# The last K-transposed-V slice padded from 64 to 128 rows, its four pairs in one place, and routing one step later

## Chip, cores and metric

The kernel runs on one core of one Trainium2 chip. The metric is the device time of one execution in microseconds (us); lower is better.

## What is computed

Three layers follow one another on 4608 tokens (8 batches of 576) of width 512. In the reference, cut to what matters:

```python
kv = np.einsum('bhsd,bhse->bhde', k, v)          # linear attention, 8 heads of 64
out = np.einsum('bhsd,bhde->bhse', q, kv)
x = out / sqrt(mean(out * out, -1) + 1e-06) * g_norm
h = np.maximum(np.maximum(x @ w1, x @ w2), x @ w3)   # first MoE: 512 -> 768 -> 512
x = h @ w_out
noisy_logits = x @ w_gate + log1p(exp(x @ w_noise)) * noise   # second MoE: 8 experts
# the two best experts of each token, with weights from their logits
h = np.maximum(x[mask] @ w1[e], 0.0)
out[mask] += top2_w[mask, k, None] * (h @ w2[e])
```

## The kernel before

The tokens go through the first two layers in nine chunks of 512 (`c` = 0 to 8). Each engine runs its instructions in the order in which the program text issues them; tiles and semaphores decide only how long one waits.

A chunk has 18 steps (`g` = 0 to 17), and then a window. In step `g` the function `g1` makes one product for the first MoE: 12 matmuls of 128 rows and 512 columns into one of four PSUM banks (`hbank`, used in turn). ScalarE (ACT) or VectorE (DVE) then empties the bank into `hm`: line 307 for the first of three products, line 309 for the other two, and lines 312 and 313 split the result into a high and a low part. So a bank that a product took is wanted again four bank requests later. The window holds the second product of the first MoE (`g2`, line 327), and the attention output of the next chunk (`ao`, `norm`, `xtrans`).

`misc1(c, g)` is called ahead of each `g1(c, g)` and puts the other work of a chunk between the steps:

- Step 0: the loads of `q` of the next chunk and of K and V of batch `c + 1`. A batch has 576 rows, which are four slices of 128 and a last one of 64 rows. Two slices go to the tile `KV0`, two to one of the three tiles `STG` (named `G` in the profile), and the 64 rows to another. `stage` hands out the three in turn.
- Step 1: `route_a` of the chunk before: DVE finds the two best experts of each token, and their one-hot sums `Mb` and `Cb` (lines 365 to 368).
- Step 3: `route_b`: two small bf16 matmuls on PE (lines 379 and 380) count the tokens, and DVE makes row numbers from them (lines 382 to 386). `scatter(c - 1, 0)` behind it has GpSimd (POOL) issue four indirect DMAs (line 393) that write the rows of the first choice to `Xg`.
- Step 7: `scatter(c - 1, 1)` for the second choice. It begins with a DVE copy into `rows` (line 401), the tile that the first four DMAs read.
- Steps 8, 9, 11 and 12: `kv_pair(c + 1, p, ...)`, five fp32 matmuls for each of four pairs of heads (line 180), which are ten instructions on PE. The fifth is the 64-row slice. `kv_out` after step 12's pair copies the result to `KB`.
- Steps 14 and 16: `ao` and `norm` for half of the next chunk.

Chunk 0 also converts the first MoE's weights from float64 (`conv_a`, `conv_b`: lines 417 to 435, on DVE, ACT and POOL), and holds batch 1's matmuls: slices 0 to 3 ahead of steps 3 to 6, the 64-row slice ahead of step 9, with all four pairs side by side. Batch 0 stands in the prologue, slice by slice. The three tiles `STG` are also used by `gate_a` and `gate_b` in chunk 0's window (lines 445 to 458). `fills` issues POOL's instructions that set `tri` and `base`, and then the DMA that fills `out` with zeros (line 496) and a part of `Xg` (line 498); it stands at chunk 1, step 0, but POOL has little else to do then and runs ahead.

The second MoE (phase 2) follows with a table of work units that is built at run time, and the experts' products on PE (lines 900, 914 and 947).

Of the kernel before, what the change touches and what calls it, by code (L numbers as in the profile page):

```python
# [17 lines left out]
NB, NH, S, D = 8, 8, 576, 64  # L18
# [57 lines left out]
def unit_order():  # L76
    seq = [("S", 0), ("S", 1), ("4", 0)]
    small = [("1", i) for i in range(N1_MAIN)] + [("2", i) for i in range(N2)]
    for i in range(1, N4):
        seq.append(("4", i))  # L80
        seq.append(small.pop(0))
    return seq + small, [("1", i) for i in range(N1_MAIN, N1)]


def body(tc, A, dbg=None):
    nc = tc.nc
    PE, ACT, DVE, POOL, SP = nc.tensor, nc.scalar, nc.vector, nc.gpsimd, nc.sync
# [8 lines left out]
    def st(name, shape, dt=F):  # L96
        return sb.tile(shape, dt, name=name)
# [4 lines left out]
    STG = [st(f"G{i}", [128, 2048]) for i in range(3)]  # L102
# [5 lines left out]
    XN = [st(f"xn{i}", [128, 512]) for i in range(3)]  # L108
# [17 lines left out]
    def abank():  # L126
        cnt["a"] += 1
        return AC[(cnt["a"] - 1) % 4]

    def C(name, a=0, b=None):  # L130
        lo, hi = CST[name]
        return cst[:, lo + a:hi if b is None else lo + b]

    ident = C("ident")

# [1 line left out]
    stg_n = [0]  # L137

    def stage(src, width=2048, parts=128):
        t = STG[stg_n[0] % 3]  # L140
        stg_n[0] += 1
        SP.dma_start(t[0:parts, 0:width], src)
        return t

    ACT.preload_act_table_set(LNEXP)
    kvraw = {}

    def quarters(t):
        return [t[:, i * 512:(i + 1) * 512] for i in range(4)]

    def load_kv(b, part):
        if part == 0:
            SP.dma_start(KV0, A["kv4"][b, 0])
            kvraw[b] = [quarters(KV0)]
        elif part == 1:
            kvraw[b].append(quarters(stage(A["kv4"][b, 1])))
        else:
            t = stage(A["kvr"][b], 1024, 64)
            kvraw[b].append((t[0:64, 0:512], t[0:64, 512:1024]))

    qbuf = [RB, KV0] + [RB] * 7

# [3 lines left out]
    def load_q(c):  # L166
        SP.dma_start(qbuf[c][:, 0:2048], A["qT"][c])

    DVE.memset(KB[0], 0.0)
    POOL.memset(KB[1], 0.0)  # L170
    POOL.memset(ones, 1.0)

# [1 line left out]
    def kv_mm(b, p, s, out):  # L174
        r = kvraw[b]
        if s < 4:
            k, v = r[s // 2][2 * (s % 2):2 * (s % 2) + 2]
        else:
            k, v = r[2]
        PE.matmul(out, k[:, p * 128:(p + 1) * 128], v[:, p * 128:(p + 1) * 128], start=s == 0, stop=s == 4)  # L180

    def kv_pair(b, p, bank):
        for s in range(5):
            kv_mm(b, p, s, bank[:, p * 128:(p + 1) * 128])

    def kv_out(b, bank):
        v = bank.rearrange("p (a e) -> p a e", a=4)
        for h in range(2):
            s = slice(h * 64, h * 64 + 64)
            (ACT.copy if h else DVE.tensor_copy)(KB[b % 2][s, :, s], v[s, :, s])  # L190
# [75 lines left out]
        xtrans_hi(i, t)  # L266
        xtrans_lo(i, t)

# [1 line left out]
    def split(src, w):  # L270
        ACT.activation(w[:, 0:1024], src, AF.Copy)  # L271
        DVE.tensor_tensor(w[:, 1024:2048], src, w[:, 0:1024].bitcast(F), op=OP.subtract)  # L272
# [16 lines left out]
    first = []  # L289
# [41 lines left out]
            for z in range(2):  # L331
                ACT.activation(rows[:, i, z * 256:z * 256 + 256], x2b[i][z][:, 0:256], AF.Copy)

# [1 line left out]
    lgs = st("lgs", [128, 4, 16])  # L335
    nl = st("nl", [128, 4, 8])
    m8 = st("m8", [128, 4, 8])
# [64 lines left out]
        for i in range(4):  # L402
            scatter_to(si[c % 2][:, 4 * k + i:4 * k + i + 1], rows[:, i, :])

# [1 line left out]
    w_raw = {}  # L406

    def load_w1(s):
        t = STG[stg_n[0] % 3]
        stg_n[0] += 1  # L410
        SP.dma_start(t.bitcast(U64), A["w1s"][s])
        w_raw[s] = t.rearrange("p (n t) -> p n t", t=2)
# [27 lines left out]
    def gate_a(j, ring):  # L440
        t, d = wsrc(9 + j), STG[j]
        for ff in range(2):
            TR = ring()
            for k in range(4):
                PE.transpose(TR[:, k * 128:(k + 1) * 128], t[:, ff * 512 + k * 128:ff * 512 + (k + 1) * 128], ident)
            ACT.activation(d[:, ff * 512:ff * 512 + 512], TR, AF.Copy)
# [10 lines left out]
        ACT.activation(hi, t, AF.Copy)  # L457
        DVE.tensor_tensor(lo, t, hi.bitcast(F), op=OP.subtract)

# [1 line left out]
    pad = st("pad", [128, XW])  # L461
    load_kv(0, 0)
    stg_n[0] = 2
    load_kv(0, 1)
    stg_n[0] = 1
    load_kv(0, 2)
    load_q(0)
    stg_n[0] = 0
    load_w1(0)
    SP.dma_start(cst, A["cst"][:, 0:CST["tri"][0]])  # L470
    SP.dma_start(gn, A["gn"])
# [11 lines left out]
    def kv_diag(b):  # L483
        for p in range(4):
            for h in range(2):
                s = slice(h * 64, h * 64 + 64)
                (ACT.copy if h else DVE.tensor_copy)(KB[b][s, p, s], AC[p][s, s])
# [3 lines left out]
    def fills():  # L491
        POOL.tensor_copy(tri, pad[:, 0:128])
        POOL.tensor_copy(base, C("eR"))
        POOL.memset(pad[:, 0:513], 0.0)
        DVE.tensor_copy(pad[:, 513:514], C("trash"))
        POOL.dma_start(A["out"].rearrange("(a p) f -> p a f", p=128),
                       pad[:, 0:512].unsqueeze(1).to_broadcast([128, OUT_ROWS // 128, 512]))
        POOL.dma_start(Xg[DUMMY:DUMMY + 512, :].rearrange("(a p) w -> p a w", p=128),
                       pad.unsqueeze(1).to_broadcast([128, 4, XW]))
# [29 lines left out]
    def conv_some(b, upto=0):  # L529
        budget[0] += b  # L530
        while conv and (budget[0] >= conv[0][0] or (conv_b, upto) in [x[1:] for x in conv]):
            t, f, k = conv.pop(0)
            budget[0] -= t
            f(k)
            if f is conv_b and k + 3 < 12:
                load_w1(k + 3)

# [1 line left out]
    P2 = {}  # L539
    order, rest = unit_order()  # L540
    NUN = len(order)
    state = {"split": 0, "load": 3, "g2done": -1, "NP": 4 * NUN}
# [86 lines left out]
            load_pair(state["load"])  # L629
            state["load"] += 1  # L630

# [1 line left out]
    def misc1(c, g):  # L633
        if c == 1 and g == 0:
            fills()
        if c == 0:
            if g == 16:
                assert 9 not in [x[2] for x in conv] and conv
                gate_a(0, abank)
            conv_some(CB if g < 17 else 99.0, g // 2)  # L640
            if 3 <= g < 7:
                for p in range(4):
                    if g == 3:
                        abank()
                    kv_mm(1, p, g - 3, AC[p][:, 0:128])
            if g == 5:
                kvraw[1].append([XN[z][0:64, :] for z in range(2)])
                for z in range(2):
                    SP.dma_start(XN[z][0:64, :], A["kvr"][1][:, z * 512:z * 512 + 512])
            if g == 6:  # L650
                load_q(1)
            if g == 9:
                for p in range(4):
                    kv_mm(1, p, 4, AC[p][:, 0:128])
                kv_diag(1)
        if g == 0:
            SP.dma_start(noise[c % 2], A["noise"][c])
        if g == 0 and 0 < c < NCH - 1:
            load_q(c + 1)
            if c + 1 < NB:  # L660
                for i in range(3):
                    load_kv(c + 1, i)
        if c > 0:
            if g == 1:
                route_a(c - 1)
            if g == 3:
                route_b(c - 1)
                scatter(c - 1, 0)
            if g == 7:
                scatter(c - 1, 1)  # L670
        if 0 < c < NB - 1:
            for p, gg in enumerate((8, 9, 11, 12)):
                if g == gg:
                    if p == 0:
                        P2["kvb"] = abank()
                    kv_pair(c + 1, p, P2["kvb"])
                    if p == 3:
                        kv_out(c + 1, P2["kvb"])
        if 0 < c < NCH - 1 and g in (14, 16):
            ao(c + 1, (g - 14) // 2, abank())  # L680
            norm(c + 1, (g - 14) // 2)
        if c == NCH - 1:
            if g == 5:
                spec_pick()
                load_regs(0, spi[0:1, 0:1], spi[0:1, 1:2])
                regE[1] = regE[0]
                regS[1] = SP.value_load(spi[0:1, 2:3], min_val=0, max_val=DUMMY)
                for p in range(3):
                    load_pair(p)
            if g == 9:  # L690
                load_rows(0)
            if g in (12, 13, 14, 15, 16, 17):
                splits(1)
# [56 lines left out]
            g1(c, g)  # L750
        window(c)

# [1 line left out]
    c = NCH - 1  # L754
    TS = STG[(stg_n[0] + 2) % 3]

# [107 lines left out]
        x = ui[u]  # L864
        load_regs(u, tabi[0:1, 0, x:x + 1], tabi[0:1, 1, x:x + 1])

# [1 line left out]
    hring = B1.rearrange("p (f a t) -> p f a t", f=4, a=2)  # L868
    hn = [0]
    h1 = [sb2.tile([128, 2, 256], FR, name=f"h1_{i}") for i in range(2)]  # L870
# [205 lines left out]
```

## Time and profile before

| | |
|---|---|
| device time, median of 3 runs | 1648.06 us (1647.77 to 1648.1) |
| span of the profiled execution, first to last instruction | 1651.1 us |
| mean granted TensorE clock | 0.982 |
| PE busy | 1593.1 us (96%) |
| PE weight loads | 1363.3 us (83%) |
| DVE, ACT, POOL busy | 749.0, 608.3, 278.3 us |
| DMA | 219.38 MB, mean 133 GB/s |

The profiled execution is one of its own: its span is 3.0 us longer than the median of the runs, and no device time of its own is listed. Times in rows are counted from the start of that span. PE counts as busy from a matmul's start to its modelled end, and matmuls overlap, so what one of them takes on PE is read from the distance to the next one's start. Chunk 1 starts at about 154 us, chunk 8 ends at about 775 us.

### The profile page before, as it was taken

The page shows a single profiled execution, that of the slowest core. Times are in us where ns is not written, and L with a number is a line of the kernel's source. Part 1 is how long each engine was busy: PE and PEld are TensorE (multiplying, and loading weights), DVE is VectorE, ACT ScalarE, POOL GpSimd, SP SyncE. Part 2 cuts the span into 40 slices and gives each one's busy share as a digit, 9 for nine tenths or more (in the row PEclk, how much of TensorE's full clock was granted, in tenths as well). Part 3 has the DMA queues.
Part 4 walks back from the last instruction along what each step waited for, and adds up shares of the span by engine and source line. Part 5 has one row for each costly group of instructions (what it writes and reads, how often), then busy time and mean ns, then how long its engine had stood idle before and what let it go on. Part 6 is the DMA issues. An engine that isn't in the chain of part 4 may idle for free. (4 is left out here: it accounts for less than half of the span.)

```text
span 1651.1 us, 21416 instructions
## 1 busy us (share of the span) xinstructions
PE 1593.1 (96%) x8500; PEld 1363.3 (83%) x8500; DVE 749.0 (45%) x1369; ACT 608.3 (37%) x968; POOL 278.3 (17%) x271
## 2 busy tenths in 40 slices
PE   6779999999999999999999999999999999999996
PEld 5659898988888888989788888888888888888885
DVE  6973243434333333444644355364354444544442
ACT  4443131313222222333233355454354443544433
POOL 3770201111020202020311121111020110201102
PEclk8978999999999999999999999999999999999998
DMA  7428121202030301051464575675574654746543
GB/s 269 155 87 313 52 84 51 103 33 110 26 129 7 135 8 71 1 179 37 188 191 115 141 217 164 196 208 166 154 212 132 179 166 145 219 130 183 165 122 71
DMA packets 53000, 219.38 MB, mean 133 GB/s; under 512 B 6944, under 2 KB 7200, under 8 KB 35488
## 3 DMA queue, kind: packets, MB, share of 16 engines
q1 hardware_dynamic: 33040, 166.50, 28.7%
q0 software_dynamic: 19856, 51.48, 13.3%
q8 instruction: 68, 1.11, 0.3%
q14 instruction: 36, 0.29, 0.1%
HBM read 166.49 MB, written 51.47 MB: 132 GB/s over the span
## 5 line engine op out<-in xcount | busy, mean ns | idle before, releaser
L287 PE MATMUL bank<-B,W 128*128 128x512 f32 x1944 | 466.2, 397 | 12.4 <-ACT W L434 6.8
L287 PEld LDWEIGHTS bank<-B,W 128*128 128x128 f32 x1944 | 364.2, 190 | 93.8 <-ACT W L434 10.6
L947 PE MATMUL bank<-W,B 128*128 128x512 f32 x1728 | 422.4, 391 | 2.0 <-issue 1.5
L947 PEld LDWEIGHTS bank<-W,B 128*128 128x128 f32 x1728 | 320.0, 188 | 67.8 <-issue 2.4
L900 PE MATMUL bank<-B,W 128*128 128x512 f32 (+1 forms) x1728 | 361.0, 346 | 0.0
L900 PEld LDWEIGHTS bank<-B,W 128*128 128x128 f32 x1728 | 275.7, 189 | 40.2
L272 DVE TENSOR_TENSOR W<-G,W 128x1024 fp32r<-128x1024 f32 x200 | 242.5, 1224 | 132.1 <-ACT W L271 132.1
L905 DVE SCALAR_TENSOR_TENSOR B<-bank,B 128x512 fp32r<-128x512 f32 (+1 forms) x176 | 104.3, 593 | 266.3 <-ACT B L904 265.8
L271 ACT ACTIVATE W<-G 128x1024 fp32r<-128x1024 f32 x200 | 207.6, 1054 | 47.1 <-PE bank L947 39.5
L904 ACT ACTIVATE B<-bank 128x512 fp32r<-128x512 f32 (+1 forms) x176 | 91.6, 521 | 351.2 <-PE bank L900 344.1
L327 PE MATMUL bank<-W,B 128*128 128x256 f32 (+1 forms) x1296 | 172.9, 291 | 4.0 <-ACT W L457 2.8
L327 PEld LDWEIGHTS bank<-W,B 128*128 128x128 f32 x1296 | 164.6, 192 | 5.5 <-ACT W L457 3.0
L393 POOL DMA_INDIRECT Xg<-RA,si x72 | 70.1, 973 | 566.2 <-ACT hm L307 458.7
L309 DVE TENSOR_TENSOR hm<-hm,bank 128x512 f32<-128x512 f32 x108 | 73.9, 684 | 162.1 <-PE bank L287 150.1
L953 POOL DMA_INDIRECT out<-xn,idt x37 | 59.6, 1612 | 318.6 <-ACT xn L952 178.9
L312 ACT ACTIVATE B<-hm 128x512 fp32r<-128x512 f32 x54 | 34.0, 630 | 214.1 <-DVE hm L309 195.2
L900 PE MATMUL bank<-xlo,W 128*128 128x512 f32 x384 | 105.0, 394 | 0.0
L900 PEld LDWEIGHTS bank<-xlo,W 128*128 128x128 f32 x384 | 72.0, 187 | 16.6
L602 ACT ACTIVATE B<-bank 128x512 fp32r<-128x512 f32 x76 | 45.3, 596 | 68.5 <-PE bank L598 61.7
L953 POOL DMA_INDIRECT out<-x2T,idt x19 | 30.6, 1611 | 233.4 <-ACT x2T L952 175.8
L313 DVE TENSOR_TENSOR B<-hm,B 128x512 fp32r<-128x512 f32 x54 | 43.0, 796 | 39.8 <-ACT B L312 39.1
L307 ACT ACTIVATE hm<-bank 128x512 f32<-128x512 f32 x54 | 32.2, 597 | 71.9 <-PE bank L287 62.6
(175 smaller groups left out, 1055.2 us busy)
## 6 DMA issues: line engine op xcount, KB each, us to landing
G<-mw SPq DMA_DIRECT2D x100, 1024.0 KB
RB<-Xg SPq DMA_DIRECT2D x13, 1028.0 KB
G<-w1s SPq DMA_DIRECT2D x12, 1024.0 KB
out<-pad POOLq DMA_DIRECT2D x1, 9472.0 KB
kv<-kv SPq DMA_DIRECT2D x8, 1024.0 KB
RB<-qT SPq DMA_DIRECT2D x8, 1024.0 KB
G<-kv SPq DMA_DIRECT2D x7, 1024.0 KB
RA<-Xg SPq DMA_DIRECT2D x8, 514.0 KB
```

What stands on the lines that cost most here:

```text
L271: ACT.activation(w[:, 0:1024], src, AF.Copy)
L272: DVE.tensor_tensor(w[:, 1024:2048], src, w[:, 0:1024].bitcast(F), op=OP.subtract)
L287: PE.matmul(bank, w[:, a, k, s], xT[b][:, k, :], start=n == 0 and k == 0, stop=n == 2 and k == 3)
L309: DVE.tensor_tensor(hm, hm, bank, op=OP.max)
L327: PE.matmul(x2b[i][z][:, 0:hi - lo], h[:, a, s], w[:, b, lo:hi], start=f == 0 and n == 0, stop=f == 5 and n == 2)
L393: i = POOL.indirect_dma_start(out=Xg, out_offset=bass.IndirectOffsetOnAxis(ap=idx, axis=0), in_=src, in_offset=None)
L602: ACT.activation(x[0][:, :, s], t, AF.Copy)
L900: PE.matmul(bank[:, 0:n], w[:, a, k, s], x[b][:, k, 0:n], start=z == 0, stop=z == 11)
L904: ACT.activation(h[:, 0, 0:n], bank[:, 0:n], AF.Relu)
L905: DVE.scalar_tensor_tensor(h[:, 1, 0:n], bank[:, 0:n], 0.0, h[:, 0, 0:n].bitcast(F), op0=OP.max, op1=OP.subtract)
L947: PE.matmul(obank[i], h[:, a, s], w[:, b, ff % 2, :], start=ff == 0 and n == 0, stop=ff == 7 and n == 2)
L953: POOL.indirect_dma_start(out=A["out"], out_offset=bass.IndirectOffsetOnAxis(ap=idt[u % 3][:, i:i + 1], axis=0), in_=y, in_offset=None, co ...
```

## The change

The 64-row slice becomes a slice of 128 rows. The upper 64 rows of the tiles that hold it are set to zero: by POOL for `STG[1]` at the program's start (batch 0), by DVE for the two `XN` tiles in chunk 0's step 5 (batch 1), and by POOL for `STG[2]` at chunk 1's step 0, ahead of `fills` (batches 2 to 7). So that the zeros stay, the loads of batches 2 to 7 no longer take the next tile in turn: the slices 2 and 3 go to `STG[0]` or `STG[1]`, the last one to `STG[2]`. The four pairs of batches 2 to 7 stand together ahead of step 10. `route_b` and the scatters move from steps 3 and 7 to 4 and 8.

```diff
--- before.py
+++ after.py
...
@@ -153,10 +153,13 @@
             SP.dma_start(KV0, A["kv4"][b, 0])
             kvraw[b] = [quarters(KV0)]
         elif part == 1:
-            kvraw[b].append(quarters(stage(A["kv4"][b, 1])))
+            t = STG[2 if b == 0 else b % 2]
+            SP.dma_start(t, A["kv4"][b, 1])
+            kvraw[b].append(quarters(t))
         else:
-            t = stage(A["kvr"][b], 1024, 64)
-            kvraw[b].append((t[0:64, 0:512], t[0:64, 512:1024]))
+            t = STG[1 if b == 0 else 2]
+            SP.dma_start(t[0:64, 0:1024], A["kvr"][b])
+            kvraw[b].append((t[:, 0:512], t[:, 512:1024]))
 
     qbuf = [RB, KV0] + [RB] * 7
 
@@ -166,11 +169,12 @@
     def load_q(c):
         SP.dma_start(qbuf[c][:, 0:2048], A["qT"][c])
 
+    POOL.memset(STG[1][64:128, 0:1024], 0.0)
     DVE.memset(KB[0], 0.0)
     POOL.memset(KB[1], 0.0)
     POOL.memset(ones, 1.0)
 
     def kv_mm(b, p, s, out):
         r = kvraw[b]
         if s < 4:
...
@@ -457,15 +461,12 @@
         ACT.activation(hi, t, AF.Copy)
         DVE.tensor_tensor(lo, t, hi.bitcast(F), op=OP.subtract)
 
     pad = st("pad", [128, XW])
     load_kv(0, 0)
-    stg_n[0] = 2
     load_kv(0, 1)
-    stg_n[0] = 1
     load_kv(0, 2)
     load_q(0)
-    stg_n[0] = 0
     load_w1(0)
     SP.dma_start(cst, A["cst"][:, 0:CST["tri"][0]])
     SP.dma_start(gn, A["gn"])
@@ -535,8 +536,7 @@
             if f is conv_b and k + 3 < 12:
                 load_w1(k + 3)
 
-    P2 = {}
     order, rest = unit_order()
     NUN = len(order)
     state = {"split": 0, "load": 3, "g2done": -1, "NP": 4 * NUN}
@@ -629,9 +629,10 @@
             load_pair(state["load"])
             state["load"] += 1
 
     def misc1(c, g):
         if c == 1 and g == 0:
+            POOL.memset(STG[2][64:128, 0:1024], 0.0)
             fills()
         if c == 0:
             if g == 16:
@@ -644,8 +645,9 @@
                         abank()
                     kv_mm(1, p, g - 3, AC[p][:, 0:128])
             if g == 5:
-                kvraw[1].append([XN[z][0:64, :] for z in range(2)])
+                kvraw[1].append([XN[z][:, :] for z in range(2)])
                 for z in range(2):
+                    DVE.memset(XN[z][64:128, :], 0.0)
                     SP.dma_start(XN[z][0:64, :], A["kvr"][1][:, z * 512:z * 512 + 512])
             if g == 6:
                 load_q(1)
@@ -663,19 +665,16 @@
         if c > 0:
             if g == 1:
                 route_a(c - 1)
-            if g == 3:
+            if g == 4:
                 route_b(c - 1)
                 scatter(c - 1, 0)
-            if g == 7:
+            if g == 8:
                 scatter(c - 1, 1)
-        if 0 < c < NB - 1:
-            for p, gg in enumerate((8, 9, 11, 12)):
-                if g == gg:
-                    if p == 0:
-                        P2["kvb"] = abank()
-                    kv_pair(c + 1, p, P2["kvb"])
-                    if p == 3:
-                        kv_out(c + 1, P2["kvb"])
+        if 0 < c < NB - 1 and g == 10:
+            bank = abank()
+            for p in range(4):
+                kv_pair(c + 1, p, bank)
+            kv_out(c + 1, bank)
         if 0 < c < NCH - 1 and g in (14, 16):
             ao(c + 1, (g - 14) // 2, abank())
             norm(c + 1, (g - 14) // 2)
...
@@ -864,7 +863,7 @@
         x = ui[u]
         load_regs(u, tabi[0:1, 0, x:x + 1], tabi[0:1, 1, x:x + 1])
 
     hring = B1.rearrange("p (f a t) -> p f a t", f=4, a=2)
     hn = [0]
     h1 = [sb2.tile([128, 2, 256], FR, name=f"h1_{i}") for i in range(2)]
```

PE's order in chunk 1, the stretch with the pairs. `G` are the `STG` tiles, `kv` is `KV0`; a row here is one fp32 matmul (two instructions in the profile), and `waits` names the engine or DMA queue whose semaphore it waits for. Before:

```order
L287 MATMUL bank_105<-B_84,W_73 128x512 [waits DVE_49]
L287 MATMUL bank_105<-B_84,W_73 128x512 x11
L180 MATMUL bank_111<-kv_91 128x128 x2
L180 MATMUL bank_111<-G_81 128x128 x2
L180 MATMUL bank_111<-G_82 128x128
L287 MATMUL bank_106<-B_84,W_73 128x512 [waits DVE_49]
L287 MATMUL bank_106<-B_84,W_73 128x512 x11
L287 MATMUL bank_107<-B_84,W_74 128x512 [waits Activation_49]
L287 MATMUL bank_107<-B_84,W_74 128x512 x11
L180 MATMUL bank_111<-kv_91 128x128 x2
L180 MATMUL bank_111<-G_81 128x128 x2
L180 MATMUL bank_111<-G_82 128x128
```

Of the change:

```order
L184 MATMUL bank_111<-kv_91 128x128 x2
L184 MATMUL bank_111<-G_81 128x128 x2
L184 MATMUL bank_111<-G_83 128x128
L184 MATMUL bank_111<-kv_91 128x128 x2
L184 MATMUL bank_111<-G_81 128x128 x2
L184 MATMUL bank_111<-G_83 128x128
L291 MATMUL bank_107<-B_84,W_74 128x512 [waits Activation_49]
L291 MATMUL bank_107<-B_84,W_74 128x512 x11
```

The last slice is the `G_82` row of a pair before and the `G_83` row now. Before, one product of 12 matmuls or two stand between two pairs (here the second and the third); now the four pairs follow one another (here the third and the fourth), and step 10's product comes behind them. Only the first pair waits for its loads, before and now.

PE's order in chunk 1 around the routing. Before:

```order
L287 MATMUL bank_105<-B_84,W_69 128x512 x12
L287 MATMUL bank_106<-B_84,W_70 128x512 x12
L379 LDWEIGHTS onesb
L379 MATMUL bank_107<-Cb,onesb 128x40 [waits DVE_49]
L380 LDWEIGHTS trib [waits Pool_49]
L380 MATMUL bank_107<-Mb,trib 128x32
L287 MATMUL bank_104<-B_84,W_70 128x512 [waits Activation_49]
L287 MATMUL bank_104<-B_84,W_70 128x512 x11
L287 MATMUL bank_105<-B_84,W_71 128x512 [waits DVE_49]
L287 MATMUL bank_105<-B_84,W_71 128x512 x11
```

Of the change:

```order
L291 MATMUL bank_106<-B_84,W_70 128x512 x12
L291 MATMUL bank_107<-B_84,W_70 128x512 x12
L383 LDWEIGHTS onesb [waits DVE_49]
L383 MATMUL bank_104<-Cb,onesb 128x40 [waits Activation_49]
L384 LDWEIGHTS trib [waits Pool_49]
L384 MATMUL bank_104<-Mb,trib 128x32
L291 MATMUL bank_105<-B_84,W_71 128x512 [waits DVE_49]
L291 MATMUL bank_105<-B_84,W_71 128x512 x11
L291 MATMUL bank_106<-B_84,W_71 128x512 [waits DVE_49]
L291 MATMUL bank_106<-B_84,W_71 128x512 x11
```

One more product stands ahead of the routing's matmul, the wait for DVE has moved to the weight load ahead of it, and the routing takes the bank of the chunk's first product (emptied by ACT). Step 4's product now takes the bank of the second one, which DVE empties.

POOL's order at the end of chunk 0's conversions and at `fills`. Before:

```order
L435 TENSOR_TENSOR W_79<-RA,W_79 128x2x512 [waits Activation_49]
L435 TENSOR_TENSOR W_80<-RA,W_80 128x2x512 [waits Activation_49]
L492 CAST trib<-pad 128x128 [waits DMAHW0_49]
L493 COPY base<-cst 128x8 [waits DMAHW5_49]
L494 MEMSET pad 128x513 [waits Pool_49]
L496 DMA out<-pad 128x37x512 [waits Pool_49]
L498 DMA Xg<-pad 128x4x514 [waits DVE_49]
```

Of the change:

```order
L439 TENSOR_TENSOR W_79<-RA,W_79 128x2x512 [waits Activation_49]
L439 TENSOR_TENSOR W_80<-RA,W_80 128x2x512 [waits Activation_49]
L635 MEMSET G_83 64x1024 [waits PE_49,Activation_49,Pool_49]
L493 CAST trib<-pad 128x128 [waits DMAHW0_49,Pool_49]
L494 COPY base<-cst 128x8 [waits DMAHW5_49]
L495 MEMSET pad 128x513 [waits Pool_49]
L497 DMA out<-pad 128x37x512 [waits Pool_49]
L499 DMA Xg<-pad 128x4x514 [waits DVE_49]
```

POOL's memset of `STG[2]` (`G_83`), which waits for PE, stands ahead of the instructions of `fills`.

## Rows read from the trace of the kernel before

**Rows 1.** The page: PE's busy time; PE's clock in 40 slices, in tenths.

```profile
PE 1593.1 (96%) x8500; PEld 1363.3 (83%) x8500; DVE 749.0 (45%) x1369; ACT 608.3 (37%) x968; POOL 278.3 (17%) x271
...
PEclk8978999999999999999999999999999999999998
```

**Rows 2.** Windows, one chunk: stretch, length, PE, PEld, DVE, ACT, POOL busy; clock; DMA.

```profile
155.90:234.80 78.90, 78.49 (x453) 68.58 (x452) 29.06 (x85) 20.29 (x43) 8.51 (x16) 1.00 0.22 82
```

**Rows 3.** Waits of PE: us in total, times, the longest.

```profile
PE bank L379 <- DVE Cb L368: 3.3, 8, 0.4
```

**Rows 4.** Timeline of PE, first and last 64-row place (start, us); group of those rows.

```profile
175.55 0.61 PE L180 MATMUL bank<-kv 128*128 128x128 f32 x4
176.32 0.28 PE L180 MATMUL bank<-G 128*128 128x128 f32 x1
176.53 0.37 PE L180 MATMUL bank<-G 64*128 64x128 f32 x1
176.74 0.27 PE L180 MATMUL bank<-G 64*128 64x128 f32 x1
176.94 0.50 PE L287 MATMUL bank<-B,W 128*128 128x512 f32 x1
177.28 0.39 PE L287 MATMUL bank<-B,W 128*128 128x512 f32 x1
...
586.73 0.27 PE L180 MATMUL bank<-G 64*128 64x128 f32 x1
587.26 0.39 PE L287 MATMUL bank<-B,W 128*128 128x512 f32 x1
...
L180 PE MATMUL bank<-G 64*128 64x128 f32 x56 | 12.8, 317 | 0.0
```

**Rows 5.** Timeline of PE, 64-row passes of batch 0.

```profile
11.43 0.94 PE L180 MATMUL bank<-G 64*128 64x128 f32 x7
```

**Rows 6.** Timeline of PE, routing of chunk 0 and the ninth routing.

```profile
160.77 0.61 PE L287 MATMUL bank<-B,W 128*128 128x512 f32 x2
161.79 0.18 PE L379 MATMUL bank<-Cb,onesb 128*128 128x40 bf16 x1 [0.41 <-DVE Cb L368]
161.84 0.48 PE L287 MATMUL bank<-B,W 128*128 128x512 f32 x1
...
778.77 0.39 PE L947 MATMUL bank<-W,B 128*128 128x512 f32 x1
779.07 0.48 PE L900 MATMUL bank<-B,W 128*128 128x512 f32 x1
```

**Rows 7.** Timeline of DVE, step 1 of chunk 1.

```profile
162.72 0.68 DVE L309 TENSOR_TENSOR hm<-hm,bank 128x512 f32<-128x512 f32 x1
```

**Rows 8.** Timeline of DVE and POOL: start, chunk 0, and line 313 in chunk 1.

```profile
0.94 0.48 DVE L169 MEMSET kvbd<- 128x512 f32 x1 [0.94 <-PEq L1068]
...
58.82 0.67 DVE L309 TENSOR_TENSOR hm<-hm,bank 128x512 f32<-128x512 f32 x1
59.03 2.45 POOL L421 TENSOR_TENSOR G<-RB,G 128x1024 int32<-128x1024 int32 x1 [1.21 <-issue]
60.64 1.38 DVE L313 TENSOR_TENSOR B<-hm,B 128x512 fp32r<-128x512 f32 x1 [1.14 <-ACT B L312]
...
164.89 0.69 DVE L313 TENSOR_TENSOR B<-hm,B 128x512 fp32r<-128x512 f32 x1 [0.70 <-ACT B L312]
```

**Rows 9.** Timeline of POOL, PE, DVE around the fill; windows: last three clock, DMA, GB/s.

```profile
120.31 2.19 POOL L496 DMA_DIRECT2D out<-pad  x1 [0.33 <-POOL pad L494]
133.48 1.85 PE L453 MATMUL bank<-wgn,G 128*128 128x16 f32 x16
174.29 0.17 DVE L401 COPY RA<-wt 128x4 f32<-128x4 f32 x1 [1.91 <-DMA Xg<-RA,si]
...
125.00:130.00 5.00, 5.00 (x25) 5.00 (x25) 0.19 (x1) 1.37 (x3) 0.00 (x0) 0.50 1.01 374
145.00:150.00 5.00, 5.00 (x45) 5.00 (x43) 2.99 (x6) 2.09 (x5) 0.00 (x0) 1.00 1.01 419
```

## The prediction

> **What bounds the kernel now.** I read the page first, then PE's waits, the stages by windows, and only then single instructions. PE is busy for 1593.1 us of the span, and its clock is below full speed only in the first four slices (digits 8, 9, 7, 8) and the last one [rows 1]. The windows show a middle chunk: PE busy in 78.49 of 78.90 us at clock 1.00, DMA at 0.22 [rows 2]. So in chunks 1 to 8 a microsecond taken from PE's instructions or waits comes off the end, as long as no other wait appears. In the list of waits only one belongs to these chunks: line 379, 3.3 us in 8 times, released by DVE's `Cb` [rows 3]. Chunk 0 is another stage: there DVE and POOL convert weights, and PE's own time is worth little.
>
> The 0.41 us before `Cb` was known. What the list of waits does not show is the price of the 64-row slice: PE counts as busy there, and one must read start times.
>
> **The 64-row slice.** Batches 2 to 7 have four pairs each, so 24 places where two 64-row passes (an fp32 matmul is two instructions) stand between 128-row work. In the first one the 128-row passes start 0.11 us apart (seven steps from 175.55 to 176.32). Then: 0.21 to the first 64-row pass, 0.21 to the second, 0.20 to the next product's matmul, and 0.34 to the one after that [rows 4]. Together 176.32 to 177.28, 0.96 us. With 128 rows I expect three steps of 0.11 and one of a 512-column matmul, 0.22 to 0.23 (two of them take 0.61, one 0.39 [rows 6]): 0.56 us. The excess is 0.40 us. The last place shows the same: 586.73 to 587.26 is 0.53, and in the first place 176.74 to 177.28 is 0.54. The group of 56 rows is 28 matmuls, 4 of them of batch 0, which leaves the 24 [rows 4]. 24 x 0.40 = 9.6, with rounding 9.4 to 9.6; I take **9.5 us**.
>
> Do 128 rows cost more per pass than 64? In batch 0 the 64-row passes stand together: seven starts within 0.94 us, of which the last one's 0.27 goes off, so 0.11 us a step [rows 5], as with 128 rows. The padded passes cost nothing by this row.
>
> The Trainium skill, TensorEngine Tiling (Array Packing), section Theoretical Speedup, speaks against the change: a dimension of at most 64 can bring up to a factor of two by tiling, which padding would give up. By that rule the 64 passes would be dearer by half a step each, 3.5 us in all. Rows 5 do not bear it out, since these 64-row passes all sit on the same rows of the array and none overlaps another.
>
> **The four pairs together.** They move from before steps 8, 9, 11 and 12 to before step 10. Forty passes at 0.11 us are 4.4 us in one piece, no more than in four. The loads they need are issued at the chunk's start, so the first pair gets two steps more (5.5 us) of time. The copy to `KB` comes two steps earlier, and its readers stay at step 14. Alone, this part is worth nothing.
>
> **Routing one step later.** Before: the last matmul ahead of it starts at 160.99 (160.77 plus 0.22), the next product's at 161.84: 0.85 us, with 0.41 of idle put down to `Cb` [rows 6]. The ninth routing, in the second MoE, has no wait: 778.77 to 779.07, 0.30 us [rows 6]. So one costs 0.55 us more than it must. One more product (12 x 0.23 = 2.7 us) ahead of it covers that five times. 8 x 0.55 = **4.4 us**. The DVE instructions behind the routing stood behind line 313 of step 2 anyway (164.89 to 165.58 [rows 8]), 3 us after PE's routing, so tables and scatters keep their times.
>
> **Chunk 0.** The prologue's four last matmuls lose about 0.2 us on the chain to the first copies of `KB` (two steps of 0.21 that become 0.11): **-0.2**. Batch 1's group at step 9 saves PE as much, which waits for the conversions there: nothing. POOL's memset of `G` at the start is hidden, since PE reads it only after 11 us [rows 5]. DVE gets two memsets of 64x512 ahead of line 309 of step 5. The nearest row is 0.48 us for 128x512 [rows 8]; two are 0.97. Line 309 starts at 58.82, line 313 at 60.64 and ends at 62.02, because POOL's addition holds until 61.48; undisturbed, line 313 takes 0.69 [rows 8]. Shifted by 0.97 it starts at 61.61, after POOL's end, and ends at 62.30: **+0.3**. That is one end. The other: the second memset, too, waits for POOL's end; then line 309 starts at about 61.95, line 313 at 63.77, ending at 64.46: +2.4. I take the first, because line 309 itself runs beside the same POOL instruction in 0.67 us [rows 8], and a memset reads less than it.
>
> The Trainium skill, SBUF — State Buffer, section Who interferes with whom, has the rule for it: a DVE instruction with at most one SBUF input, outside the two-port modes, does not contend with GpSimd. By it the term is 0.3; if memset were in such a mode it would be 2.4. No row shows a DVE memset beside a POOL instruction that reads.
>
> **The fill of `out`.** POOL's memset of `STG[2]` must wait for `gate_b(2)`, which reads that tile until 133.48 + 1.85 = 135.33 [rows 9]. Behind it in POOL's queue stand `tri`, `base`, `pad` and the fill, now issued at 120.31 [rows 9]. With about 1 us for the memset (twice the columns of the 0.48) and about 1.7 for the small ones (an estimate: 0.5 for a memset of 513 columns, the rest alike) it goes out at 138, 18 us later, and its data, after an issue of 2.19, from about 141. 9.7 MB of `out`, 1.05 of `Xg` and 2.4 MB of loads of batch 2 run at 374 GB/s or a little more [rows 9]: 35 us, to about 176. The scatters of chunk 0 stand behind it in the same queue and land by about 179. Who waits for them: DVE's copy of `rows` (1.91 us already now, at 174.29 [rows 9]), at step 8 instead of 7. PE's step 8 ends near 177.7 (step 4 begins at 164.0, see the rivals, and five steps take 13.7); its bank is wanted again at step 12, at about 190 (step 9, 4.4 us of pairs, steps 10 and 11). Ten microseconds of cover: nothing. `tri` is ready at 138, and is wanted at 164.
>
> **Sum.** -9.5 -4.4 -0.2 +0.3 = -13.8 us. The profiled span of 1651.1 would be 1637.3. The runs have a median of 1648.06, 3.0 us under that span; the terms are PE time at full clock and carry over, so 1648.06 - 13.8 = **1634.3 us**.
>
> **Rivals.**
> *The excess is not of the 64 rows* but of the change of tile or the semaphores there. Against: 128-row passes step from `kv` to `G` without a break [rows 4]. Then only routing gains: 1643.8.
> *Routing's wait comes back a step later*, on the bank: step 4's product now takes the bank that line 309 of step 1 empties at 162.72 + 0.68 = 163.40 [rows 7]. PE gets there at 161.84 - 0.55 + 2.7 = 164.0. Half a microsecond of room; if it is used up in all chunks, 4.4 come back: 1638.7.
> *Chunk 0 is dearer*: the memset takes its upper end (+2.1), and a stretch of chunk 0 at 1.2 instead of 2.4 GHz grows with it. The three microseconds between the profiled execution and the runs suggest some 2 us for that: 1638.4.
> *The padding costs* the 3.5 us of the tiling rule as a mechanism of the array: 1637.8.
> *Slower, by one mechanism*: the late fill. If fill and loads move at half the rate, the scatters land at about 141 + 70 = 211, DVE stands at the copy until then, and PE waits for step 8's bank from 190 on: 21 us, so 1655. From 204 on this decides the sign. The trace has 1.01 of DMA share and 419 GB/s with both kinds of transfer in flight [rows 9], which speaks against it.
>
> **How the numbers follow.** The forecast gets 0.78, chunk 0 dearer 0.12, the wait on the bank 0.04, the excess elsewhere 0.03, the padding 0.01, the late fill 0.02. The range: the forecast less up to 3 us, because chunk 0's half-speed stretches may also shrink (estimate from the same 3.0 us), and up to chunk 0's dear case: 1631.3 to 1638.6. A measurement here tells 0.2%, 3.3 us, from nothing. All cases but the last stay below 1644.8, only the excess elsewhere comes near: faster 0.95, same 0.03, slower 0.02.
>
> **What would show it.** After: no step over 0.13 us within the forty passes, the first product's matmul behind them 0.11 later and then 0.23 apart; chunks 1 to 6 shorter by 4 x 0.40 + 0.55 = 2.1 us (78.9 to 76.8), chunks 7 and 8 by 0.55; no wait at the routing in PE's list, and none at step 4; line 313 after the memsets ending 0.3 later; the fill issued at about 138 and no PE wait in chunk 1. Wrong would be: padded passes above 0.11, a PE wait before step 4 or 12, or chunk 1's routing more than 2 us away from 164.0.

## The result and the profile after

| | before | after |
|---|---|---|
| device time, median | 1648.08 us (1647.77 to 1651.56, 4 runs) | 1632.56 us (1632.25 to 1636.84, 4 runs) |
| ratio | | 0.9902, 95% interval 0.9887 to 0.9917 |
| span of the profiled execution | 1651.1 us | 1630.4 us (device time of this run 1632.4) |
| mean granted TensorE clock | 0.982 | 0.986 |

The change makes the kernel 15.5 us faster; 1634.3 was forecast, 13.8 us less. The page, by the lines of [rows 1]:

```profile
PE 1575.4 (97%) x8500; PEld 1354.4 (83%) x8500; DVE 748.6 (46%) x1371; ACT 608.6 (37%) x968; POOL 280.6 (17%) x273
...
PEclk9979999999999999999999999999999999999998
```

The busy time of PE fell by 17.7 us, which is more than the change is worth: the clock's digits of the first slices read 9, 9, 7, 9 where they read 8, 9, 7, 8 before, so chunk 0 also ran at a higher clock in this execution. A better measure is the distance between the same instruction in two chunks. The routing, by the rows of [rows 6]:

```profile
159.24 0.39 PE L291 MATMUL bank<-B,W 128*128 128x512 f32 x1
159.47 0.19 PE L383 MATMUL bank<-Cb,onesb 128*128 128x40 bf16 x1
159.54 0.48 PE L291 MATMUL bank<-B,W 128*128 128x512 f32 x1
...
236.00 0.19 PE L383 MATMUL bank<-Cb,onesb 128*128 128x40 bf16 x1
```

Before, chunk 1's routing matmul starts at 161.79 [rows 6], and chunk 2's at:

```profile
240.56 0.18 PE L379 MATMUL bank<-Cb,onesb 128*128 128x40 bf16 x1 [0.41 <-DVE Cb L368]
```

Now they start at 159.47 and 236.00: a chunk takes 76.53 us, where it took 78.77. The routing itself has no idle time in brackets any more; from the matmul ahead of it to the next product's it takes 159.24 to 159.54, 0.30 us instead of 0.85. The pairs of batch 2, by the rows of [rows 4]:

```profile
175.50 0.61 PE L291 MATMUL bank<-B,W 128*128 128x512 f32 x2
175.96 0.61 PE L184 MATMUL bank<-kv 128*128 128x128 f32 x4
176.40 0.83 PE L184 MATMUL bank<-G 128*128 128x128 f32 x6
177.07 0.61 PE L184 MATMUL bank<-kv 128*128 128x128 f32 x4
177.52 0.83 PE L184 MATMUL bank<-G 128*128 128x128 f32 x6
178.19 0.61 PE L184 MATMUL bank<-kv 128*128 128x128 f32 x4
178.63 0.83 PE L184 MATMUL bank<-G 128*128 128x128 f32 x6
179.30 0.61 PE L184 MATMUL bank<-kv 128*128 128x128 f32 x4
179.75 0.83 PE L184 MATMUL bank<-G 128*128 128x128 f32 x6
180.34 0.94 PE L291 MATMUL bank<-B,W 128*128 128x512 f32 x3
```

The passes of the four pairs follow one another without a step that stands out: the 20 from 177.07 to 179.30 take 0.11 us each, the padded ones among them. The PE list of waits (us in total, times, the longest) begins with:

```profile
PE bank L449 <- DVE RA L432: 7.4, 1, 7.4
PE bank L256 <- issue: 6.9, 1, 6.9
PE bank L291 <- ACT W L438: 6.1, 3, 3.5
PE bank L184 <- DMA kv<-kv: 5.7, 1, 5.7
```

The row of `Cb` from [rows 3] is gone, and nothing took its place: all these lie in the prologue and in chunk 0.

### The profile page after: what moved, and what is told of

Same layout as the page of the kernel before. It is cut to its first block, busy times and chain, and to the rows that moved or that the text cites. A ratio compares the mean times of both kernels' runs of the same rounds, so it can differ in the third digit from the quotient of the medians.

```text
span 1630.4 us, 21416 instructions
## 1 busy us (share of the span) xinstructions
PE 1575.4 (97%) x8500; PEld 1354.4 (83%) x8500; DVE 748.6 (46%) x1371; ACT 608.6 (37%) x968; POOL 280.6 (17%) x273
## 5 line engine op out<-in xcount | busy, mean ns | idle before, releaser
L291 PE MATMUL bank<-B,W 128*128 128x512 f32 x1944 | 458.7, 395 | 12.4 <-ACT W L438 6.1
L952 POOL DMA_INDIRECT out<-hm,idt x19 | 30.1, 1585 | 165.3 <-ACT hm L951 66.1
```

Source lines behind the costliest of these rows:

```text
L291: PE.matmul(bank, w[:, a, k, s], xT[b][:, k, :], start=n == 0 and k == 0, stop=n == 2 and k == 3)
L952: POOL.indirect_dma_start(out=A["out"], out_offset=bass.IndirectOffsetOnAxis(ap=idt[u % 3][:, i:i + 1], axis=0), in_=y, in_offset=None, co ...
```

## The experiments

The times of the first four kernels stand against 1649.63 us, the median of 19 runs of the kernel before that were taken beside them; those of the last four against 1650.03 us (14 runs).

### The padding alone

Tiles, memsets and loads as in the change; pairs and routing where they were.

```diff
-            kvraw[b].append(quarters(stage(A["kv4"][b, 1])))
+            t = STG[2 if b == 0 else b % 2]
+            SP.dma_start(t, A["kv4"][b, 1])
+            kvraw[b].append(quarters(t))
...
-            t = stage(A["kvr"][b], 1024, 64)
-            kvraw[b].append((t[0:64, 0:512], t[0:64, 512:1024]))
+            t = STG[1 if b == 0 else 2]
+            SP.dma_start(t[0:64, 0:1024], A["kvr"][b])
+            kvraw[b].append((t[:, 0:512], t[:, 512:1024]))
...
+    POOL.memset(STG[1][64:128, 0:1024], 0.0)
...
+            POOL.memset(STG[2][64:128, 0:1024], 0.0)
             fills()
...
+                    DVE.memset(XN[z][64:128, :], 0.0)
...
```

Expected:

> The padding alone (128 rows, zeros, fixed tiles for the loads); the pairs stay at steps 8, 9, 11 and 12 and the routing at 3 and 7. If the excess is of the change between 64 and 128 rows, 24 places give 24 x 0.40 = 9.5 us: 1638.6 us, and chunks 1 to 6 are shorter by 1.6 each. If it is of the change of tile or of the semaphores there, nothing: 1648. If the padded passes cost more, less than 9.5.

Measured: 1640.59 us, ratio 0.995 (0.9936 to 0.9964). PE's timeline, the routing of chunks 1 and 2:

```profile
158.05 0.18 PE L383 MATMUL bank<-Cb,onesb 128*128 128x40 bf16 x1 [0.41 <-DVE Cb L372]
...
235.27 0.18 PE L383 MATMUL bank<-Cb,onesb 128*128 128x40 bf16 x1 [0.41 <-DVE Cb L372]
```

The chunk takes 77.22 us, 1.55 less than before, and so do all of chunks 1 to 6: 9.3 us, or 0.39 for each of the 24 places. Chunks 7 and 8, which have no pairs, keep their length. The 0.41 us behind `Cb` stays. So the excess is of the 64 rows.

### The routing alone

```diff
-            if g == 3:
+            if g == 4:
                 route_b(c - 1)
                 scatter(c - 1, 0)
-            if g == 7:
+            if g == 8:
                 scatter(c - 1, 1)
```

Expected:

> Routing and scatters one step later, and nothing else. If the wait for Cb is the whole price, 8 x 0.55 = 4.4 us: 1643.7 us, chunks 1 to 8 shorter by 0.55 each. If the wait comes back on the bank of step 4, nothing: 1648.

Measured: 1645.27 us, ratio 0.9973 (0.9963 to 0.9983). PE's timeline:

```profile
159.54 0.19 PE L379 MATMUL bank<-Cb,onesb 128*128 128x40 bf16 x1
...
237.75 0.19 PE L379 MATMUL bank<-Cb,onesb 128*128 128x40 bf16 x1
```

The chunk takes 78.21 us, 0.56 less, and each of the eight chunks is shorter by 0.55 or 0.56: 4.43 us together. The wait behind `Cb` is gone.

### The pairs together, with 64 rows

```diff
-        if 0 < c < NB - 1:
-            for p, gg in enumerate((8, 9, 11, 12)):
...
+        if 0 < c < NB - 1 and g == 10:
+            bank = abank()
+            for p in range(4):
+                kv_pair(c + 1, p, bank)
+            kv_out(c + 1, bank)
```

Expected:

> The four pairs together ahead of step 10, with 64-row slices, routing as before. If the price is of the change of rows, each pair still pays it twice, and the time stays: 1648, within 1 us. If standing between products is what costs, most of the 9.5 us goes: 1639.

Measured: 1649.09 us, ratio 0.9998 (0.9989 to 1.0007): no difference that the device time shows. PE's timeline does show one:

```profile
158.41 0.18 PE L379 MATMUL bank<-Cb,onesb 128*128 128x40 bf16 x1 [0.40 <-DVE Cb L368]
...
237.04 0.18 PE L379 MATMUL bank<-Cb,onesb 128*128 128x40 bf16 x1 [0.40 <-DVE Cb L368]
```

78.63 us is 0.14 less than the 78.77 of before, and the six chunks together are 0.85 us shorter. Each pair still pays its steps of 0.20, 0.21, 0.20 and 0.21 around the 64-row passes, now against the next pair's 128-row passes.

### 64 rows, but side by side

The four pairs of a batch slice by slice, in four banks, so that the eight 64-row passes follow one another. No padding.

```diff
...
+        if 0 < c < NB - 1 and g == 10:
+            banks = [abank() for p in range(4)]
+            for s in range(5):
+                for p in range(4):
+                    kv_mm(c + 1, p, s, banks[p][:, 0:128])
+            for p in range(4):
+                for h in range(2):
+                    s = slice(h * 64, h * 64 + 64)
+                    (ACT.copy if h else DVE.tensor_copy)(KB[(c + 1) % 2][s, p, s], banks[p][s, s])
```

Expected:

> No padding, but the four 64-row slices of a batch stand side by side ahead of step 10, each pair in a bank of its own (eight small copies instead of two); routing as before. If the price is of the change of rows, three of four places go in each of six batches: 18 x 0.40 = 7.2 us less, 1640.9. If it is of each 64-row pass, nothing: 1648.

Measured: 1643.42 us, ratio 0.9962 (0.9949 to 0.9975). PE's timeline, first the routing of chunks 1 and 2, then the 64-row passes of batch 2:

```profile
158.80 0.18 PE L379 MATMUL bank<-Cb,onesb 128*128 128x40 bf16 x1 [0.40 <-DVE Cb L368]
...
236.27 0.18 PE L379 MATMUL bank<-Cb,onesb 128*128 128x40 bf16 x1 [0.40 <-DVE Cb L368]
```

```profile
181.66 0.37 PE L180 MATMUL bank<-G 64*128 64x128 f32 x1
181.88 0.94 PE L180 MATMUL bank<-G 64*128 64x128 f32 x7
182.75 0.50 PE L287 MATMUL bank<-B,W 128*128 128x512 f32 x1
```

The chunk takes 77.47 us, 1.30 less, 7.8 us in six. The group of seven spans 0.94 us with its last pass's 0.27, so its steps are 0.11: a 64-row pass costs what a padded one does. The first step is 0.22 (181.66 to 181.88) and the next product starts at 182.75. What is paid is the change between 64 and 128 rows, once for a chunk here and four times before: three such changes of 0.39 are 1.17 us, and with the 0.14 of the pairs' place 1.31. This version keeps the loads as they were. A chunk gains less from it than from padding and the new place together, 1.30 against 1.55 + 0.14 us, because one change to 64 rows and back is left.

### The kernel before and the change once more

Both unchanged, each with a second trace.

Expected:

> The kernel before once more, for a second trace of it. The time stays within 0.2%. If the stop of PE of some 2 us in the second MoE (no semaphore, 27 us after chunk 8's end) belongs to the program, it is there again; if it is an accident of one execution, it is not. If chunk 0's half-speed stretches vary from execution to execution, chunk 0 ends up to 5 us away from 153.2.

> The changed kernel once more, for a second trace: 1632.6 against 1648.1 of the first comparison. If the missing stop in the second MoE belongs to the program, it is missing again, and chunk 8's end to the span's end is 881.1 again; if not, about 883.

Measured: 1650.06 us, ratio 0.9998 (0.9988 to 1.0008), and 1635.28 us, ratio 0.9908 (0.9894 to 0.9922). The lengths of chunks 1 to 8 are those of the first traces: 615.06 and 615.07 us in the two of before, 600.52 in both of the change. The other stretches differ between executions of one program. Windows of the change, 120 to 125 us, in its first trace and in its second (stretch, length, PE, PEld, DVE, ACT, POOL busy, clock, DMA share, GB/s):

```profile
120.00:125.00 5.00, 5.00 (x36) 5.00 (x35) 0.00 (x0) 0.00 (x0) 0.00 (x0) 0.76 0.00 0
```

```profile
120.00:125.00 5.00, 5.00 (x25) 5.00 (x25) 0.00 (x0) 0.00 (x0) 0.00 (x0) 0.53 0.00 0
```

The clock is 0.76 in the one and 0.53 in the other, and chunk 1's first product starts at 148.57 and 149.78. Over ten traces it starts between 148.57 and 153.52 us, with 153.04 and 149.76 for the two of before. The other stretch is about 28 us behind chunk 8's end. PE's timeline in the first trace of the change, in the second of before, and in the second of the change:

```profile
774.70 2.89 PE L946 MATMUL bank<-W,B 128*128 128x512 f32 x12
```

```profile
793.26 0.49 PE L947 MATMUL bank<-W,B 128*128 128x512 f32 x1 [0.85 <-issue]
794.68 0.86 PE L947 MATMUL bank<-W,B 128*128 128x512 f32 x3 [0.94 <-issue]
```

```profile
778.78 0.40 PE L946 MATMUL bank<-W,B 128*128 128x512 f32 x1 [0.22 <-issue]
780.20 0.38 PE L598 MATMUL bank<-cst,RB 128*128 128x128 f32 x2 [0.79 <-issue]
```

In the first PE goes on from matmul to matmul; in the second it stands for 0.85 and 0.94 us, and in the third for 0.22 and 0.79, put down to "issue", so to nothing that the profile shows. POOL issues the scatters of the pads there, in the trace without a stop as well. The first trace of before and all the other experiments have such a stop. What makes it is open; no run was made for it.

So the two first spans differ by 20.7 us for three reasons: 14.54 in chunks 1 to 8, 4.5 in chunk 0 (153.04 against 148.57), and 1.7 behind chunk 8. Only the first is the change's, but for some 0.2 us of chunk 0 (below). The device times are 15.5 us apart in the result and 14.75 here (1650.03 against 1635.28).

### The fill of `out` ahead of the memset

The change, with POOL's memset of `STG[2]` behind the fills instead of ahead of them.

```diff
         if c == 1 and g == 0:
-            POOL.memset(STG[2][64:128, 0:1024], 0.0)
             fills()
+            POOL.memset(STG[2][64:128, 0:1024], 0.0)
```

Expected:

> The changed kernel with POOL's memset of STG[2] behind the fill instead of ahead of it, so that the fill goes out some 15 us earlier again. If the late fill is hidden, DVE's 7.8 us at the copy of rows shrink to about 2 and the time stays that of the change, within 0.2%. If the late fill costs, it is faster by more.

Measured: 1635.04 us, ratio 0.9907 (0.9893 to 0.9921), the change's 0.9908 again. POOL's timeline at the fill, and DVE's at the copy into `rows`:

```profile
120.00 2.19 POOL L497 DMA_DIRECT2D out<-pad  x1 [0.33 <-POOL pad L495]
```

```profile
172.77 0.17 DVE L405 COPY RA<-wt 128x4 f32<-128x4 f32 x1 [0.49 <-DMA Xg<-RA,si]
```

The fill goes out at 120.00 instead of 133.23, and the copy waits for 0.49 us. Chunk 1 takes 76.53 us as in the change. So the late fill of the change is hidden.

### The fill issued twice

The change, with a second fill of `out` behind the first.

```diff
         POOL.dma_start(A["out"].rearrange("(a p) f -> p a f", p=128),
                        pad[:, 0:512].unsqueeze(1).to_broadcast([128, OUT_ROWS // 128, 512]))
+        POOL.dma_start(A["out"].rearrange("(a p) f -> p a f", p=128),
+                       pad[:, 0:512].unsqueeze(1).to_broadcast([128, OUT_ROWS // 128, 512]))
```

Expected:

> The changed kernel with the zero fill of out issued twice (9.7 MB more, about 24 us at 0.4 MB per us). The rival's mechanism is forced: the first scatters land near 203, DVE stands at the copy of rows, and PE waits at step 12 from about 186 on, some 17 us: 1649 to 1651. If DVE's stand does not reach PE, the time stays at 1632.6.

Measured: 1661.06 us, ratio 1.0059 (1.0042 to 1.0076), 25.8 us above the change. Chunk 1 takes 101.90 us, 25.4 more. POOL's timeline, DVE's, PE's waits, and the windows (columns as above):

```profile
138.16 2.18 POOL L497 DMA_DIRECT2D out<-pad  x1 [0.33 <-POOL pad L495]
173.60 2.00 POOL L499 DMA_DIRECT2D out<-pad  x1 [33.26 <-DMA out<-pad]
...
206.68 1.04 POOL L397 DMA_INDIRECT Xg<-RA,si  x1 [30.24 <-DMA Xg<-pad]
```

```profile
213.46 0.17 DVE L405 COPY RA<-wt 128x4 f32<-128x4 f32 x1 [37.04 <-DMA Xg<-RA,si]
```

```profile
PE bank L291 <- DVE hm L313: 23.3, 1, 23.3
```

```profile
194.30:214.30 20.00, 0.00 (x0) 0.00 (x0) 0.79 (x2) 0.01 (x1) 4.69 (x9) 0.50 0.67 254
214.30:218.30 4.00, 3.99 (x10) 3.18 (x11) 2.39 (x4) 2.00 (x4) 3.34 (x7) 0.53 0.34 132
```

The chain is the one of the slower rival. The second fill was issued only at 173.60, because POOL waits 33.26 us for the first to land (both write `out`); the first scatter waits another 30.24 for the fill of `Xg`; DVE stands at the copy for 37.04 us, until 213.46; and PE stands for 23.3, from 191.0 to 214.3. In that wait the granted clock falls to 1.2 GHz (0.50 from 194.3 on), and the first 4.0 us behind it still have 0.53, which loses about 4.0 x 0.47 = 1.9 us more. The sum is 25.2 of the chunk's 25.4. The mechanism was as expected, and the size, some 17 us, was not: the second fill's wait for the first (the DMA share is 0.03 from 172 to 176 us) and the clock behind the stop both came on top.

## Why the prediction was right, step by step

| term, us | forecast | measured | from |
|---|---|---|---|
| 64-row slice, 24 places | -9.5 | -9.3 | padding alone: 6 x 1.55 |
| four pairs together | 0 | -0.85 | pairs together: chunks 1 to 6 |
| routing, 8 chunks | -4.4 | -4.43 | routing alone |
| chunk 0: prologue, memsets | +0.1 | +0.18 | end of the conversions, one pair of traces |
| sum | -13.8 | -14.4 | |

The three parts add up: 1.55 + 0.14 + 0.555 = 2.245 a chunk, where the whole change shows 2.24.

**The 64-row slice.** Right in place and size: 0.39 for 0.40 a place. One detail came otherwise: behind the last padded pass the product's first matmul starts after 0.03 us and the next one 0.31 later, where 0.11 and 0.23 were forecast; the sum is the same. What costs is the change of the number of rows, and the rows themselves cost nothing, as the 64-row passes side by side and the padded passes show, 0.11 a step for both. The Trainium skill, TensorEngine Tiling (Array Packing), section Theoretical Speedup, gives up to a factor of two for a dimension of at most 64. It is not seen here: 64-row passes that all use the same rows of the array start no closer than 128-row ones.

**The pairs together.** The step "Alone, this part is worth nothing" is the mis-sized term: it is worth 0.85 us, too little for the device time of the single part, but plain in each of the six chunks. Only one product, not four, stands behind a pair's passes then. By starts alone, not by a run of its own: the second to the twelfth matmul of a product are 0.230 us apart on average behind a pair before, and 0.227 behind another product. Over eleven steps that is about 0.04 us a product, and three products a chunk make some 0.12 of the 0.14.

**Routing.** Right, 0.55 a chunk. Forecast was that PE comes to step 4's product at 164.0; it comes at 159.54, which is 164.0 less the 4.5 us by which chunk 0 ended sooner. There is no wait at it. By the letter one of the forecast's signs of being wrong is met, since the routing of chunk 1 lies more than 2 us from 164.0. The sign was set as a time from the span's start, and chunk 0 alone moves that by up to 5 us; counted from chunk 1's start the forecast fits.

**Chunk 0.** The lower end of the memsets' cost was the right one. DVE's timeline, and POOL's:

```profile
59.11 1.02 DVE L650 MEMSET xn<- 64x512 f32 x2 [0.16 <-issue]
60.16 0.69 DVE L313 TENSOR_TENSOR hm<-hm,bank 128x512 f32<-128x512 f32 x1
61.55 0.69 DVE L317 TENSOR_TENSOR B<-hm,B 128x512 fp32r<-128x512 f32 x1 [0.70 <-ACT B L316]
```

```profile
59.08 2.45 POOL L425 TENSOR_TENSOR G<-RB,G 128x1024 int32<-128x1024 int32 x1 [1.22 <-issue]
```

The two memsets take 1.02 us inside POOL's instruction (59.08 to 61.53), so they do not wait for it; line 317, which is [rows 8]'s line 313, ends at 62.24 instead of 62.02: +0.22 for a forecast of +0.3. By the Trainium skill, SBUF — State Buffer, section Who interferes with whom, a DVE instruction with at most one SBUF input, outside the two-port modes, does not contend with GpSimd. The trace agrees. The prologue's -0.2 cannot be read: its passes lost the steps of 0.20 and 0.22 us, but the first copy to `KB` starts at 11.74 us before and at 11.73 now, and over ten traces anywhere from 11.13 to 12.90. By the end of the conversions (line 458 at 119.15 before, the same instruction as line 462 at 119.33 now) the stage is 0.18 us later in this pair of traces. What chunk 0 really does to a time is its clock: its end moves by up to 5 us between executions. No effect of the change on that is seen, since chunk 1 starts between 148.57 and 153.52 us in the five traces with padding and between 148.63 and 153.04 in the five without.

**The fill of `out`.** Issue and wait, by POOL's and DVE's timelines:

```profile
131.01 0.95 POOL L635 MEMSET G<- 64x1024 f32 x1 [12.15 <-PE bank L457]
...
133.23 2.19 POOL L497 DMA_DIRECT2D out<-pad  x1 [0.33 <-POOL pad L495]
...
172.18 1.05 POOL L397 DMA_INDIRECT Xg<-RA,si  x1 [21.93 <-DVE hm L313]
```

```profile
179.23 0.17 DVE L405 COPY RA<-wt 128x4 f32<-128x4 f32 x1 [7.76 <-DMA Xg<-RA,si]
179.34 0.69 DVE L313 TENSOR_TENSOR hm<-hm,bank 128x512 f32<-128x512 f32 x1
```

The fill went out at 133.23, not 138, since chunk 0 ended sooner and with it the read of `gate_b(2)`. The copy comes at 179.23, for a forecast of about 179, after DVE has stood 7.76 us. That this fits is luck in part: the fill started 4.8 us sooner than forecast, and the path from the landed fill to the copy took 7.05 us (172.18 to 179.23) where 3 were forecast. The first scatter is issued at 172.18; the view names DVE as its releaser, but DVE had been done for 9 us (with the early fill the same scatter goes out at 163.67), and it is the landing of the fill that it waits for, as its row in the doubled fill says. The forecast had ten microseconds of cover. The doubled fill shows where it ends: there PE starts to wait at 191.0 (190 was forecast) in a trace whose chunk 1 starts at 153.52. In the first trace of the change, 4.95 us sooner, that is 186. Less the 0.85 us from the copy to PE's start (213.46 to 214.31 there), some 6 us are left behind the copy at 179.23. Four of the forecast's ten went, since the copy did not come sooner with chunk 0.

**From span to device time.** The 3.0 us between the profiled span and the median were taken as chunk 0's clock. The two traces of before bear that out: their spans differ by 3.4 us (1651.1 and 1647.7), 3.3 of it ahead of chunk 1, and from 124 to 132 us the granted clock is 0.50 in the first and 1.00 in the second. But the distance is more than 3.0 us. In the other runs of kernels with 64-row slices the device time is 2.2 to 2.6 us above the span, so the profiled execution of before would be at about 1653.5, some 5 us above the median. Subtracting the sum from the median, not from the span, kept that out of the forecast.

In all runs of the kernels with padded slices the device time is only 1.9 to 2.0 us above the span. So about 0.45 us of the gain lies outside the spans, and the forecast has no term for it; what it is stays open. With it the measured 14.4 become some 14.9 us, for 15.5 in the result and 14.75 in the later runs.

**The rivals.** The excess of another cause falls with the padding alone, the wait a step later with 159.54, the tiling rule with 0.11. The dear chunk 0 falls with 62.24 as far as it is the memset (its upper end was 64.46); a dearer clock is not seen, as said above. The dear case is 1638.4 by its own terms, and the range's upper end has 1638.6; nothing hangs on it. The late fill is a true mechanism, some 6 us from costing time here.

## What to carry to other kernels

Busy time hides what a matmul of another shape costs: read the distance between starts around it, and if the change of shape is what is paid for, pad the odd slice, or put the odd ones side by side. A queue that is moved behind a wait can be free and still use up most of its cover: find the first instruction of a busy engine that needs what stands behind it, and measure how late it may come. Compare chunk with chunk where the ends of the span differ between executions of one program.

## What the runs showed of the hardware

64 columns behave otherwise than 64 rows. PE's timeline of the change, matmuls of 64 columns:

```profile
130.79 1.09 PE L208 MATMUL bank<-kvbd,kv 128*64 128x128 f32 x16
```

Sixteen start within 1.09 us, less some 0.27 for the last one's run: about 0.055 us a step, half of the 0.11 of the 128-row and the 64-row passes on the same 128 columns of data. They start two by two, 0.006 to 0.007 us apart, so two of them seem to run beside each other; no run was made for it.

At both changes of the number of rows the matmul is late, and its weight load starts with it, not one matmul ahead. In the second trace of before the load of the last 128-row pass starts at 172.926, 0.11 us ahead of the pass at 173.035. The load of the first 64-row pass starts at 173.238 and the pass at 173.239; behind the 64-row passes the product's first load starts at 173.652 and its matmul at 173.654. This is read from starts: that the late load makes the price is likely, but no run takes it apart.
